# Issuing the Q and K weight loads from the scalar queue, with tiles 2 and 3 gated on tiles 0 and 1, in an attention-plus-GLU kernel

## The chip, the cores and the metric

The kernel runs on one core of a Trainium2 chip. The metric is the device time of one execution in microseconds (us).

Two numbers are used for one execution. The *time* is what is compared. The *span* runs from the first to the last instruction that the profile shows.

Engines are named as the profile names them: PE is TensorE, DVE is VectorE, ACT is ScalarE, POOL is GpSimd, SP is SyncE. "ACTq" or "SPq" is the instruction stream of that engine at work on issuing a DMA.

## The reference

One token tensor x of 2048 x 640 in bf16 is normalised. Two branches read the result and both are added to x.

```python
def reference(A_x, A_wqkv, A_wo, B_x, B_w_gate, B_w_up, B_w_down):
    def _A_ref(x, wqkv, wo):                    # 32 heads of 20, window of 8 positions, dilation 2
        # ... q, k, v from x @ wqkv; softmax over the window; weighted sum of v ...
        return o @ wo
    def _B_ref(x, w_gate, w_up, w_down):
        g = jnp.einsum("bsd,df->bsf", x, w_gate)
        u = jnp.einsum("bsd,df->bsf", x, w_up)
        return jnp.einsum("bsf,fd->bsd", g * u, w_down)
    x = A_x
    xn = _layernorm(x, axis=-1)
    return x + _A_ref(xn, A_wqkv, A_wo) + _B_ref(xn, B_w_gate, B_w_up, B_w_down)
```

## The kernel before

Tokens come in 16 tiles of 128. For the first tiles, the way to the first useful matmul is a chain over three engines: the tile lands; VectorE takes its statistics (two halves and an aggregate); ScalarE takes a square root, before which its stream has the load of a function table (1.28 us in the profile of before); VectorE takes the reciprocal and normalises; TensorE transposes; VectorE and ScalarE copy the transposed tile out of PSUM; TensorE multiplies it with the Q weights.

```python
def front(t):
    # ...
    yield have("x", t)
    if t == 1:
        yield have("sd", 0)
    for i in range(2):
        if t == 2 and i == 1:
            yield have("xnt", 1)
        yield Task("dve", lambda: stats(i), r=[x], prio=-1 if t == 1 and i == 0 else p)
    yield Task("dve", aggr, r=[("st", t, 1)], prio=p)
    yield Task("act", sqrt, r=[("mv", t)], prio=p - 1)          # "the root" below
    yield Task("dve", recip, r=[("sd", t)], prio=p)
    # ...
    yield Task("dve" if t < N_DVE_A else "act", apply, r=[("rstd", t), x], w=[xs], prio=p)   # normalise
    # ... five transposes on PE (trans), then the copy to XNT (part, copy) ...
```

The text of the program is not the order of the instructions. A scheduler in the kernel file runs when the program is built: it keeps a clock for each engine, models when each operation and each DMA ends, and appends the ready task of best priority to the engine's stream. On the chip that order is fixed, and in these traces an engine waits where an input is late, with what stands behind it: in e3 below, a reciprocal on VectorE whose root was done at 4.73 started only at 5.49, behind statistics that had waited 0.68 us for a tile. The DMA part of the model, with the program's own constants, is this:

```python
if dma:
    self.t[eng] = start + (0.48 if occ is None else occ)
    # ...
    self.t_data = max(self.t_data, start + 1.2) + nbytes / 280e3
    X.end = self.t_data + 0.8 + extra
```

These are the loads and the start of the program. `K.t["act"]` tells the model when ScalarE is free after its first issues and its table load.

```python
def x_load(t, eng="sp"):
    dma(XST[:, xslot(t), :], xhbm[t * TS:(t + 1) * TS, :], w=[XST[:, xslot(t), :]], name=f"xld{t}", eng=eng)
    mark("x", t)
# ...
def wqkv_load(g, lo=0, hi=NCH):
    dst = WQKV[:, WPOS[g], lo:hi, :]
    dma(dst, wqkv_src[:, lo:hi, g * D:(g + 1) * D], w=[dst], name=f"ld_wqkv{g}_{lo}")
# ...
x_load(0)
tch = A_wqkv.rearrange("(c k p) n -> k c p n", k=16, c=NCH)[:, :, 0, 0:32]
stores.append(dma(TCH[0:16], tch, w=[TCH[0:16]], name="touch", eng="act"))   # 5 KB that nobody reads
x_load(1)
wqkv_load(0, 0, 3)       # Q weights, first piece
wqkv_load(0, 3, NCH)     # Q weights, second piece
x_load(2)
wqkv_load(1, 0, 3)       # K weights
wqkv_load(1, 3, NCH)
x_load(3)
K.t["act"] = 2.1
warm(18)                 # 18 matmuls on zeros, before there is work for PE
```

Of the kernel before, what the change touches and what calls it, by code (L numbers as in the profile page):

```python
# [10 lines left out]
D = 640  # L11
NCH = 5
# [9 lines left out]
TS = 128  # L22
# [324 lines left out]
def build_kernel(nc, A_x, A_wqkv, A_wo, B_x, B_w_gate, B_w_up, B_w_down, out):  # L347
    K = Sched(nc)
# [4 lines left out]
    def sb(name, shape, dtype=BF16, at=None):  # L353
        n = mybir.dt.size(dtype)
        for s in shape[1:]:
            n *= s
        n = (n + 63) // 64 * 64
        if at is None:
            at = place[0]
            place[0] += n  # L360
        assert at + n <= 229344, (name, at + n)
        return K.sbuf(name, shape, dtype, at)
# [10 lines left out]
    NXS = 12  # L373
    XST = sb("XST", [128, NXS, D], at=a_ot + NCH * JB * 2)
# [43 lines left out]
    XNS = sb("XNS", [128, NXN, D], at=a_xr)  # L418
# [3 lines left out]
    MV = sb("MV", [128, NT, 2], FP32)  # L422
    SD = sb("SD", [128, NT, 4], FP32)
    DUM = sb("DUM", [128, 16], FP32)
    TCH = sb("TCH", [128, NCH, 32])
    ZERO = sb("ZERO", [128, JB])
    EPSC = sb("EPSC", [128, 16], FP32)
    IDENT = sb("IDENT", [128, 128])
# [15 lines left out]
    def mark(*k):  # L444
        done.add(k)
# [4 lines left out]
    def have(*k):  # L450
        return lambda: k in done
# [4 lines left out]
    xhbm = A_x[0]  # L456
    ohbm = out[0]

    def dma(o, i, r=(), w=(), name="", eng="sp", group=None):
        n = mybir.dt.size(o.dtype)  # L460
        for s in o.shape:
            n *= s
        return op(eng, lambda e: e.dma_start(o, i), r=r, w=w, dma=True, name=name, nbytes=n, group=group)  # L463
# [6 lines left out]
       r=[IDENT[:]], w=[IDENT[:]], name="ident", occ=0.4)  # L470
# [3 lines left out]
       r=[G[:]], w=[G[:]], name="g1", occ=0.3)  # L474
    op("pool", lambda e: e.affine_select(G[:], G[:], pattern=[[-4, H]], compare_op=ALU.is_ge,
                                         fill=0.0, base=0, channel_multiplier=1),
       r=[G[:]], w=[G[:]], name="g2", occ=0.3)
    op("pool", lambda e: e.memset(KT[:, :, 0:PAD], 0.0), w=[KT[:, :, 0:PAD]], name="kpad", occ=0.3)

    def xslot(t):  # L480
        return t + 4 if t < 8 else t - 8

    def x_load(t, eng="sp"):
        dma(XST[:, xslot(t), :], xhbm[t * TS:(t + 1) * TS, :], w=[XST[:, xslot(t), :]], name=f"xld{t}", eng=eng)
        mark("x", t)

    wqkv_src = A_wqkv.rearrange("(c p) n -> p c n", p=128)

    def wqkv_load(g, lo=0, hi=NCH):
        dst = WQKV[:, WPOS[g], lo:hi, :]  # L490
        dma(dst, wqkv_src[:, lo:hi, g * D:(g + 1) * D], w=[dst], name=f"ld_wqkv{g}_{lo}")

    def loads():
        def t(f, *a):
            return Task("sp", lambda: f(*a), prio=0)

        for t_ in range(4, NXS):
            yield t(x_load, t_)
        yield t(wqkv_load, 2)
        for t_ in range(NXS, NT):  # L500
            yield have("apply", t_ - NXS)
            yield t(x_load, t_)

        def w(T, src):
            dma(T[:], src.rearrange("(c p) n -> p c n", p=128), w=[T[:]], name="ld_w")

        def pads():
            z = ZERO[:, 0:PAD].unsqueeze(1).to_broadcast([128, NCH, PAD])
            dma(vscr[:, 0:PAD].rearrange("(c p) s -> p c s", p=128), z, r=[ZERO[:, 0:PAD]], w=[("vscr", "pad")], name="vpad")

        yield have("xnt", NT - 1)
        yield t(w, WG, B_w_gate)
        yield t(pads)
        yield t(w, WU, B_w_up)
# [107 lines left out]
    def warm(n):  # L622
        for _ in range(n):
            op("pe", lambda e: e.matmul(PS[:, 7, 0:QB], ZERO[:, 0:128], ZERO[:, 0:QB], start=True, stop=True),
               r=[ZERO[:]], w=[PS[:, 7, :]], name="warm", occ=0.2 if n > 3 else 0.12)
# [576 lines left out]
    stores = []  # L1202
# [76 lines left out]
    FIN_PRIO = 8  # L1279

    x_load(0)
    tch = A_wqkv.rearrange("(c k p) n -> k c p n", k=16, c=NCH)[:, :, 0, 0:32]
    stores.append(dma(TCH[0:16], tch, w=[TCH[0:16]], name="touch", eng="act"))
    x_load(1)
    wqkv_load(0, 0, 3)
    wqkv_load(0, 3, NCH)
    x_load(2)
    wqkv_load(1, 0, 3)
    wqkv_load(1, 3, NCH)
    x_load(3)  # L1290
    K.t["act"] = 2.1
    warm(18)

    def misc():
        yield have("xnt", NT - 1)

        def sel():
            for q in range(4):
# [6 lines left out]
                                     name="exp_preload", occ=1.3), prio=6)  # L1305

    K.spawn(loads())
    for t in range(NT):
        K.spawn(front(t))
# [20 lines left out]
def bass_parallel_sum__sliding_local_dilated__glu_gated_bilinear__prompt_kernel(  # L1330
    nc, A_x, A_wqkv, A_wo, B_x, B_w_gate, B_w_up, B_w_down, out
):
    build_kernel(nc, A_x, A_wqkv, A_wo, B_x, B_w_gate, B_w_up, B_w_down, out)
# [28 lines left out]
```

## Time and profile before

| kernel before | value |
|---|---|
| time, median of 3 runs | 270.04 us (269.69 to 270.15) |
| the profiled execution | 270.63 us, span 268.9 us, granted clock 1.0 |
| PE busy | 262.7 us, 98% of the span |
| first Q weight piece: issued, landed | 1.73, 7.17 us |
| first projection matmul | 7.30 us |

The table of stretches gives, for each window in us: its length, the busy time of each engine with its number of instructions (in the order PE, PE's weight loads, DVE, ACT, POOL), the granted clock, the busy share of the DMA engines and GB/s.

```profile
0.00:7.30 7.30, 5.37 (x26) 3.41 (x27) 3.71 (x13) 2.17 (x4) 1.30 (x10) 1.00 0.71 215
7.30:20.00 12.70, 12.09 (x195) 11.69 (x196) 8.87 (x26) 6.43 (x14) 0.00 (x0) 1.00 0.81 280
80.00:140.00 60.00, 59.58 (x311) 27.08 (x310) 50.61 (x56) 21.18 (x34) 28.89 (x15) 1.00 0.58 138
```

PE is full in the middle of the kernel. What can be won lies in the first 20 us. The next view is the chain of waits that ended last, in order of time, cut to its first part: start, length, and what was done. Pieces named "issue" of 0.05 us or less are left out of the chains shown. The weight piece is on it, from its issue to its landing.

```profile
1.73 5.44 DMA WQKV<-in_A_wqkv_dram
7.17 0.14 issue
7.30 0.84 PE PS L640 x12
8.16 0.62 PE PS L640 x8
8.78 0.29 PE PS L585 x5
9.09 0.50 DVE XNT L604
9.64 1.98 PE PS L640 x32
```

ScalarE's timeline shows the other side (start, length, engine, line, operation; in brackets the idle time before it and what ended it). The table load is over at 2.54, long before the first root is wanted; tile 0's share of the copy is done at 6.55.

```profile
0.83 0.40 ACTq L463 DMA_DIRECT2D TCH<-in_A_wqkv_dram  x1
1.26 1.28 ACT L544 ACT_TABLE_LOAD   x1 [1.26 <-PEq L1347]
4.38 0.30 ACT L544 ACTIVATE SD<-MV,EPSC 128x1 f32<-128x1 f32 x1 [1.84 <-DVE MV L541]
6.17 0.38 ACT L597 ACTIVATE XNT<-PS 128x256 bf16<-128x256 bf16 x1 [1.49 <-PE PS L585]
...
10.26 0.30 ACT L544 ACTIVATE SD<-MV,EPSC 128x1 f32<-128x1 f32 x1 [0.85 <-DVE MV L541]
```

### The profile page before, as it was taken

To read this page: it belongs to the slowest core of one execution; us is meant where nothing else is said; L and a number is where in the kernel's file an instruction comes from. 1 tells how busy PE (TensorE), PEld (TensorE's weight loads), DVE (VectorE), ACT (ScalarE), POOL (GpSimd) and SP (SyncE) were. 2 spreads that over 40 slices of the span, in tenths; PEclk is the share of its full clock that TensorE was granted. 3 is DMA by queue.
4 is the path that set the end of the run, shared out by engine and by line. 5 is a ranking of instruction groups with operands and counts; after the bars stand their busy time and mean duration, and the time that the engine had idled before them with its cause. 6 is when DMAs were issued, how large, how long until landed. Compare 5 with 4: busy or idle time off the path is not lost.

```text
span 268.9 us, 4464 instructions
## 1 busy us (share of the span) xinstructions
PE 262.7 (98%) x1765; PEld 152.8 (57%) x1783; DVE 222.9 (83%) x282; ACT 105.4 (39%) x188; POOL 130.3 (48%) x81
## 2 busy tenths in 40 slices
PE   7899999999999999999999999999999999999996
PEld 5796975444444444444444445765457654676775
DVE  4678899999999997379999899999999989992212
ACT  3369998556723232245344353024430342201000
POOL 1000000000004439900199999999999879985000
PEclk9999999999999999999999999999999999999999
DMA  6954479621414998087025953465534561022201
GB/s 206 367 188 74 98 105 339 247 97 56 142 39 113 234 244 177 0 268 151 2 52 140 240 118 79 132 176 138 152 79 130 148 195 42 27 73 61 87 28 49
DMA packets 40261, 35.58 MB, mean 132 GB/s; under 512 B 15408, under 2 KB 38448, under 8 KB 40240
## 3 DMA queue, kind: packets, MB, share of 16 engines
q1 hardware_dynamic: 39424, 33.15, 45.4%
q0 software_dynamic: 576, 2.10, 3.9%
q8 instruction: 14, 0.23, 0.4%
q10 hardware_dynamic: 240, 0.05, 0.1%
q14 instruction: 7, 0.06, 0.1%
HBM read 25.07 MB, written 5.26 MB: 113 GB/s over the span
## 4 chain that ended last, share of the span: by engine, by line
PE 94%; DMA 2%; DVE 2%; issue 1%; SPq 0%; DVEq 0%
PE PS L1149 36%; PE PS L1231 28%; PE PS L640 24%; PE PS L903 3%; DMA WQKV<-in_A_wqkv_dram 2%; PE PS L1098 2%; DVE HT L1158 1%; PE PS L585 0%; DVE RS L952 0%; DVE LOG L956 0%; SPq L463 0%; DVE XNT L604 0%; DVE SM L932 0%; DVE FOUT L1244 0%; DVEq L325 0%
## 5 line engine op out<-in xcount | busy, mean ns | idle before, releaser
L1056 POOL TENSOR_TENSOR SV<-PV 128x1024 bf16<-128x1024 f32 x40 | 93.5, 2366 | 24.7 <-DVE LOG L956 18.7
L1051 DVE TENSOR_TENSOR PV<-VX,PS 128x1024 f32<-128x1024 bf16 (+1 forms) x56 | 91.8, 1670 | 0.3 <-POOL SV L1056 0.3
L640 PE MATMUL PS<-XNT,WQKV 128*128 128x512 bf16 (+2 forms) x474 | 66.4, 299 | 1.6 <-DVE XNT L604 0.6
L1149 PE MATMUL PS<-XNT,WU 128*128 128x512 bf16 x239 | 59.6, 380 | 0.2
L1149 PE MATMUL PS<-XNT,WG 128*128 128x512 bf16 x229 | 57.3, 380 | 0.7 <-issue 0.3
L640 PEld LDWEIGHTS PS<-XNT,WQKV 128*128 128x128 bf16 x480 | 43.6, 113 | 23.8 <-DVE SD L549 1.0
L1149 PEld LDWEIGHTS PS<-XNT,WU 128*128 128x128 bf16 x240 | 23.3, 98 | 28.7 <-ACT XNT L645 0.8
L1149 PEld LDWEIGHTS PS<-XNT,WG 128*128 128x128 bf16 x240 | 23.2, 98 | 28.6 <-issue 0.8
L792 DVE TENSOR_TENSOR PRD<-QT,KT 128x2048 bf16<-128x2048 bf16 x32 | 36.8, 1217 | 0.0
L1244 DVE TENSOR_TENSOR FOUT<-PS,XR 128x320 bf16<-128x320 f32 (+1 forms) x33 | 15.7, 479 | 22.2 <-PE PS L1231 22.0
L1231 PE MATMUL PS<-WD,HT 128*128 128x320 bf16 x192 | 28.7, 300 | 0.0
L645 ACT ACTIVATE HT<-PS 128x512 bf16<-128x512 f32 x24 | 14.3, 596 | 34.0 <-PE PS L1149 34.0
L1231 PE MATMUL PS<-WO,OT 128*128 128x320 bf16 (+1 forms) x165 | 27.0, 296 | 0.0
L863 POOL TENSOR_TENSOR PRF<-PRF,PRF 128x1024 f32<-128x1024 f32 x4 | 9.4, 2352 | 33.1 <-DVE PRF L837 33.0
L1107 ACT ACTIVATE OT<-PS 128x512 bf16<-128x512 f32 x20 | 10.5, 600 | 34.4 <-PE PS L1098 34.4
L922 POOL MEMSET LOG<- 32x6 bf16 (+6 forms) x7 | 0.4, 95 | 48.4 <-ACT LOG L914 48.4
L1158 DVE TENSOR_TENSOR HT<-HT,PS 128x512 bf16<-128x512 bf16 x24 | 16.3, 680 | 8.7 <-PE PS L1149 7.0
L1231 PEld LDWEIGHTS PS<-WD,HT 128*128 128x128 bf16 x192 | 18.8, 98 | 7.6
L1231 PEld LDWEIGHTS PS<-WO,OT 128*128 128x128 bf16 x165 | 15.7, 98 | 6.6 <-issue 0.8
L837 DVE TENSOR_TENSOR PRF<-PS,KT 128x1024 f32<-128x1024 f32 x16 | 19.0, 1216 | 0.4 <-DMA PRF<-PRF 0.4
L538 DVE BATCH_NORM_STATS2 STATS<-XST 128x6 f32<-128x320 bf16 x32 | 14.7, 471 | 3.0 <-DMA XST<-in_A_x_dram 3.0
L1231 PE MATMUL PS<-WD,XNT 128*128 128x320 bf16 (+1 forms) x108 | 14.6, 285 | 0.0
(58 smaller groups left out, 216.1 us busy)
## 6 DMA issues: line engine op xcount, KB each, us to landing
VX<-v_scratch SPq DMA_DIRECT2D x80, 130.0 KB, 2.9
XST<-in_A_x_dram SPq DMA_DIRECT2D x16, 160.0 KB, 6.2
v_scratch<-VST SPq DMA_DIRECT2D x4, 640.0 KB, 4.3
XR<-in_A_x_dram SPq DMA_DIRECT2D x16, 160.0 KB, 2.9
out_dram<-FOUT SPq DMA_DIRECT2D x15, 160.0 KB, 1.8
PRF<-PRF POOLq DMA_DIRECT2D x4, 512.0 KB, 8.6
WG<-in_B_w_gate_dram SPq DMA_DIRECT2D x1, 1920.0 KB, 8.6
WU<-in_B_w_up_dram SPq DMA_DIRECT2D x1, 1920.0 KB, 12.1
```

What stands on the lines that cost most here:

```text
L538: op("dve", lambda e: e.bn_stats(o, a), r=[a], w=[("st", t, i)], name=f"bn{t}_{i}", occ=0.49)
L640: op("pe", (lambda o, l, x, c, first: lambda e: e.matmul(o, l, x, start=first, stop=(c == NCH - 1)))(o, l, x, c, first), r=[l, x], w=[o], ...
L645: X = op("act", (lambda o, i: lambda e: e.activation(o, i, ACT.Copy))(o, i), r=[i], w=[o], name=name, occ=0.12 + n * 0.9e-3)
L792: op("dve", lambda e: e.tensor_tensor(s[:], qb, kv, ALU.mult), r=[q, rk], w=[s[:]], name=f"prod{j}_{r}_{c}", occ=1.15, lock=True)
L837: X = op("dve", lambda e: e.tensor_tensor(o[:], qb, kv, ALU.mult), r=[q, rk], w=[o[:]], name=f"prow{j}_{r}_{c}_{q0}", occ=1.17)
L1051: op("dve", lambda e: e.tensor_tensor(p, vw, a, ALU.mult), r=[vv] + rk, w=[p], name=f"pv{u}_{x}_{r0}", occ=0.09 + 1.1 * nr)
L1056: X = op("pool", lambda e: e.tensor_tensor(o, p[:, :, 0, :], p[:, :, 1, :], ALU.add), r=[p[:]] + tokens(), w=[o], name=f"pva{u}_{x}", occ= ...
L1107: X = op("act", (lambda o, b: lambda e: e.activation(o, PS[:, b, :], ACT.Copy))(o, b), r=[PS[:, b, :]], w=[o], name=f"oev{u}", occ=0.58)
L1149: op("pe", (lambda l, x, c: lambda e: e.matmul(PS[:, b, :], l, x, start=(c == 0), stop=(c == NCH - 1)))(l, x, c), r=[l, x], w=[PS[:, b, :] ...
L1158: X = op("dve", lambda e: e.tensor_tensor(h, h, PS[:, hold[1], :], ALU.mult), r=[h, PS[:, hold[1], :]], w=[h], name=f"h{m}_{j}", occ=0.65)
L1231: op("pe", (lambda l, x, i: lambda e: e.matmul(dst, l, x, start=(i == 0), stop=(i == n - 1)))(l, x, i), r=[l, x], w=[PS[:, b, :]], name=f" ...
L1244: X = op("dve", lambda e: e.tensor_tensor(o, PS[:, b, 0:wid], xr, ALU.add), r=[PS[:, b, :], xr], w=[o], name=f"fin{t}_{nb}", occ=0.15 + wi ...
```

## The change

The intent is to get the weights sooner: SyncE issues only token tiles, and ScalarE issues the Q and K weights at once. Tiles 2 and 3 are loaded only when tiles 0 and 1 have been normalised, which is meant to keep them out of the weights' way. The touching read goes. `[EPSC[:]]` makes ScalarE's first issue wait for a memset, which ends at 1.24.

```diff
     def x_load(t, eng="sp"):
-        dma(XST[:, xslot(t), :], xhbm[...], w=[XST[:, xslot(t), :]], name=f"xld{t}", eng=eng)
+        r = [XNS[:, t - 2, :]] if 2 <= t < 4 else []
+        dma(XST[:, xslot(t), :], xhbm[...], r=r, w=[XST[:, xslot(t), :]], name=f"xld{t}", eng=eng)
 # ... wqkv_load gets eng= and r= ...
-        for t_ in range(4, NXS):
+        for t_ in range(2, NXS):
+            if t_ < 4:
+                yield have("apply", t_ - 2)
             yield t(x_load, t_)
 # ...
     x_load(0)
-    tch = A_wqkv.rearrange("(c k p) n -> k c p n", k=16, c=NCH)[:, :, 0, 0:32]
-    stores.append(dma(TCH[0:16], tch, w=[TCH[0:16]], name="touch", eng="act"))
     x_load(1)
-    wqkv_load(0, 0, 3)
-    wqkv_load(0, 3, NCH)
-    x_load(2)
-    wqkv_load(1, 0, 3)
-    wqkv_load(1, 3, NCH)
-    x_load(3)
-    K.t["act"] = 2.1
+    wqkv_load(0, 0, 3, "act", [EPSC[:]])
+    wqkv_load(0, 3, NCH, "act")
+    wqkv_load(1, 0, 3, "act")
+    wqkv_load(1, 3, NCH, "act")
+    K.t["act"] = 4.2
```

More of the change, by code (lines that the diff above doesn't have):

```diff
@@ L424, in build_kernel @@
     DUM = sb("DUM", [128, 16], FP32)
-    TCH = sb("TCH", [128, NCH, 32])
     ZERO = sb("ZERO", [128, JB])
@@ L483, in x_load, with wqkv_load @@
     def x_load(t, eng="sp"):
-        dma(XST[:, xslot(t), :], xhbm[t * TS:(t + 1) * TS, :], w=[XST[:, xslot(t), :]], name=f"xld{t}", eng=eng)
+        r = [XNS[:, t - 2, :]] if 2 <= t < 4 else []
+        dma(XST[:, xslot(t), :], xhbm[t * TS:(t + 1) * TS, :], r=r, w=[XST[:, xslot(t), :]], name=f"xld{t}", eng=eng)
         mark("x", t)
     wqkv_src = A_wqkv.rearrange("(c p) n -> p c n", p=128)
-    def wqkv_load(g, lo=0, hi=NCH):
+    def wqkv_load(g, lo=0, hi=NCH, eng="sp", r=()):
         dst = WQKV[:, WPOS[g], lo:hi, :]
-        dma(dst, wqkv_src[:, lo:hi, g * D:(g + 1) * D], w=[dst], name=f"ld_wqkv{g}_{lo}")
+        dma(dst, wqkv_src[:, lo:hi, g * D:(g + 1) * D], r=r, w=[dst], name=f"ld_wqkv{g}_{lo}", eng=eng)
     def loads():
```

## The prediction

> **What bounds it now.** TensorE. The page gives PE 262.7 us busy of a 268.9 us span (98%), and the chain that ended last is 94% PE. In the table of stretches PE is busy 59.6 of 60 us from 80 to 140 and again from 140 to 200. So the kernel can gain only where PE idles, and the change touches only the first 20 us. There the table shows 1.93 us idle before 7.30 (1.27 of it before the first warm-up matmul) and 0.61 us from 7.30 to 20. The opening chain (waits in order of time): SP issues x0 at 0.82, x1 at 1.27, the first Q weight piece at 1.73; that piece lands 5.44 us later, at 7.17, and the first projection matmul starts at 7.30. PE waits 0.5 us for it (waits view). The other input of that matmul, tile 0 transposed, was complete at 6.55 (timeline: ScalarE copy 6.17 + 0.38). So the weight piece is late by about 0.65 us; the rest of the start is the token chain: landing 3.2, statistics, root at 4.38, normalise 4.91, transpose 5.42, copies to 6.55.
>
> **What the change does.**
> - Q/K weights are issued by ScalarE after the memset that ends at 1.23, not by SP at 1.73: about 0.45 us earlier. [...] this 0.45 us is just that, the SP issue of x1 (0.40 us) being what is skipped.
> - Tile 2 (160 KB) no longer sits between Q and K weights, tile 3 no longer before tile 4; K weights, landing at 9.8 and 10.7 now, should land by about 8.5 to 9.5. Tile 2 is issued at about 5.4 and competes for the engines with the K weights, landing about 8.3 (8.5 now); tile 3 is issued at 7.5, landing about 10 (11.2 now).
> - ScalarE now issues four loads (0.43 to 0.49 us each by the trace) ahead of its table load (1.28 us): 1.26 + about 1.9 + 1.28 = 4.45, against a root that started at 4.38. So the token chain slips 0.1 us, more if an issue blocks (SP's later issues took 0.92 us).
> - The touching read (5 KB, landed at 3.4) goes. If it warmed the way to the weights, the first piece will be slower; in the trace 15 of its 16 engine completions were in by about 5.8 and one came at 7.17, so such stragglers exist even with it. I expect no large loss.
>
> **On the critical path.** First matmul at the later of tokens (about 6.7) and weight (5.3 to 6.8): I estimate 6.8, 0.5 us earlier. The 0.57 us gap before tile 1's projection (9.07 to 9.64, copy and transpose of tile 1) stays; its copy now goes ahead of tile 2's statistics, which helps slightly. Afterwards PE runs full, so the gain passes to the end. Reordering later (weight products among projections) moves nothing of PE's sum.
>
> **Predicted time**: 269.5 us (before 270.04), 268.7 to 270.3 eight times in ten. Faster by over 2%: 0.01; within 2%: 0.98; slower by over 2%: 0.01.
>
> **What would show it.** Right: first projection matmul at 6.6 to 7.0; its releaser ScalarE's or VectorE's tile 0 copy, not a weight; table load ending 4.3 to 4.6; K weights landed before 9.6; no PE wait for a token tile. PE busy sum unchanged within 1 us.
>
> **What would make it wrong.** ScalarE issue blocking past 5 us (root late); the first weight piece landing at 7.2 or later without the touch (gain zero or negative); tiles 2 to 4 starving PE at 12 to 16 us; a new wait in mid-kernel from the changed order of products.

One clause is cut where it is marked: a general reason for the 0.45 us, which no measurement of this case shows. No term of the prediction's sums goes with it: the root is still put at 1.26 + about 1.9 + 1.28 = 4.45, the first matmul 0.5 us earlier, the time at 269.5.

## More of the kernel before

The profiled execution was itself slower than the highest of the three timed runs.

PE reaches tile 3's transposes without a wait (no bracket):

```profile
14.54 0.45 PE L585 MATMUL PS<-IDENT,XNS 128*128 128x128 bf16 x5
```

## The result, and the profile after

The kernel after took 270.75 us (median of 6 runs, 270.55 to 270.96) where the kernel before took 270.12 us in the same rounds (6 runs, 269.69 to 270.40). The ratio is 1.0022, 95% interval [1.001, 1.0035]. A ratio here is the mean time of one kernel's fast runs over that of the other's of the same rounds, so it is not quite the ratio of the medians quoted. The result is correct, all runs were fast and the clock was 1.0 (0.999 in one). It is within 2%, as predicted, but on the wrong side of zero and outside the predicted range of 268.7 to 270.3.

The chain of waits of the kernel after, cut to its pieces up to tile 3, reads quite differently:

```profile
1.27 0.46 ACTq L462
...
2.81 0.51 ACTq L462
3.35 1.28 ACT L546
4.65 0.30 ACT SD L546
...
6.48 1.31 PE PS L642 x20
...
8.65 4.09 PE PS L642 x65
...
13.13 0.49 DVE XNT L606
13.62 0.41 DVE STATS L540
14.05 0.22 DVE MV L543
14.30 0.30 ACT SD L546
14.82 0.46 DVE XNS L558
15.32 0.45 PE PS L587 x5
```

Two things are to be seen. First, no DMA is left on it: the Q piece landed at 5.47 and the wait for it is gone. In its place stand ScalarE's four issues and then the table load, and the first root starts at 4.65, the moment the table is there (3.35 + 1.28 = 4.63). Second, there is a detour at 13.13 that the chain of before does not have: PE waits for tile 3, whose statistics stand behind a copy of tile 2 on VectorE. PE's timeline has that wait:

```profile
15.32 0.45 PE L587 MATMUL PS<-IDENT,XNS 128*128 128x128 bf16 x5 [0.34 <-DVE XNS L558]
```

PE's weight loads also waited 0.30 us, until 13.67, for that copy of tile 2. ScalarE's and VectorE's timelines show an ordering of the same kind for tile 2:

```profile
11.12 0.60 ACT L647 ACTIVATE KT<-PS 128x512 bf16<-128x512 f32 x1 [0.52 <-PE PS L642]
11.61 0.28 ACT L546 ACTIVATE SD<-MV,EPSC 128x1 f32<-128x1 f32 x1
```

```profile
9.97 0.21 DVE L543 BATCH_NORM_AGGREGATE MV<-STATS 128x2 f32<-128x12 f32 x1
11.93 0.16 DVE L551 RECIPROCAL SD<-SD 128x1 f32<-128x1 f32 x1 [1.75 <-ACT SD L546]
```

Tile 2's aggregate is done at 10.18 (9.97 + 0.21). Its root starts at 11.61, because a K evacuation stands before it in ScalarE's stream and waits for PE. The table of stretches:

```profile
0.00:7.30 7.30, 5.22 (x41) 3.71 (x42) 3.62 (x13) 2.26 (x4) 1.30 (x10) 1.00 0.74 240
7.30:20.00 12.70, 11.73 (x185) 10.85 (x183) 8.17 (x23) 5.83 (x14) 0.00 (x0) 1.00 0.85 262
```

From 7.30 to 20 PE is idle for 0.97 us (12.70 - 11.73), against 0.61 before. The span of the profiled run, 268.8, is the same as that of the profiled run of before, 268.9, though the times differ by 0.6 us in the median. Either the profiled run of before was not typical, or something lies outside the span. The experiments show both.

### The profile page after: what moved, and what is told of

Read it like the earlier page. It is cut to its first block, busy times and chain, and to the rows that moved or that the text cites. A ratio compares the mean times of both kernels' runs of the same rounds, so it can differ in the third digit from the quotient of the medians.

```text
span 268.8 us, 4476 instructions
## 1 busy us (share of the span) xinstructions
PE 263.3 (98%) x1783; PEld 152.2 (57%) x1783; DVE 223.1 (83%) x282; ACT 105.1 (39%) x188; POOL 130.3 (48%) x81
## 3 DMA queue, kind: packets, MB, share of 16 engines
q10 hardware_dynamic: 1488, 1.68, 1.8%
## 4 chain that ended last, share of the span: by engine, by line
PE 96%; DVE 1%; ACTq 1%; ACT 1%; issue 0%
PE PS L1151 39%; PE PS L1233 28%; PE PS L642 24%; PE PS L905 3%; PE PS L1100 2%; PE PS L587 1%; ACTq L462 1%; ACT L546 0%; DVE XNT L606 0%; DVE XNS L558 0%; ACT SD L546 0%; DVE STATS L540 0%; DVE SD L551 0%; PE PS L626 0%; DVE FOUT L1246 0%
## 5 line engine op out<-in xcount | busy, mean ns | idle before, releaser
L1151 PE MATMUL PS<-XNT,WG 128*128 128x512 bf16 x240 | 59.7, 379 | 0.0
```

Source lines behind the costliest of these rows:

```text
L1151: op("pe", (lambda l, x, c: lambda e: e.matmul(PS[:, b, :], l, x, start=(c == 0), stop=(c == NCH - 1)))(l, x, c), r=[l, x], w=[PS[:, b, :] ...
```

## The experiments

Fourteen kernels were run, in four batches; each batch shares its runs of the kernel before. All results were correct. Three theories stood at the start, and a fourth came out of the first batch.

- Theory A: the profiled execution of before was unlucky. Its late weight piece (one packet of 1280 bytes took 2.05 us in the trace's packet records) is not what a typical run has, so the change had less to win than the 0.65 us that the prediction read off.
- Theory B: four issues ahead of the table load delay the root by more than predicted.
- Theory C: taking the touching read away cost something.
- Theory D, later: the order that the scheduler fixed is what loses inside the kernel.

### The kernel before again, and the touching read

`e1_before_again` is the kernel before, unchanged, to get a second profile of it.

> The kernel before, unchanged, profiled and timed once more. Theory A (the first profile was unlucky: one stalled packet of 2.05 us made the first Q weight piece late, 7.17 us, and that execution took 270.63 against a median of 270.04): here the piece lands by about 5.8, the first projection matmul starts at 6.3 to 6.7, and the span is 268.1 to 268.5. Theory B (the piece is late in every execution of the kernel before): it lands again after 7.0, first projection at 7.2 or later, span 268.9. Theory C (the 0.6 us lie outside the span, before or after it): the span is again about 268.9 while the time stays at 270.1.

It took 270.04 us (269.86 to 270.98), ratio 1.0005 [0.9991, 1.0018], span of the profiled run 268.2. Its chain and PE's timeline:

```profile
1.73 4.68 DMA WQKV<-in_A_wqkv_dram
```

```profile
6.54 1.51 PE L640 MATMUL PS<-XNT,WQKV 128*128 128x128 bf16 x20 [0.48 <-DMA WQKV<-in_A_wqkv_dram]
```

The same DMA took 4.68 us instead of 5.44, and the first projection started at 6.54, not 7.30. Nor is this one profile the only evidence: the ten fast runs of before in the same rounds have spans of 267.8 to 268.6, against 268.9, and in the other kernels that issue this piece at 1.73 it landed at 6.29 (f3), 6.70 (f1) and 5.51 (f4). So the whole gain that the prediction saw (7.30 to 6.8) was there in an ordinary run of the kernel before. The kernel after starts its first projection at 6.48, earlier than e1 by 0.06 us. Theory A holds, though the piece landed at 6.41, not by 5.8: even an ordinary run of before waits about half a microsecond for it.

`f3_no_touch` is before without the touching read; `e2_touch_back` is after with it.

```diff
# f3, against before                       # e2, against after
-    stores.append(dma(TCH[0:16], tch, ... name="touch", eng="act"))
                                          +    stores.append(dma(TCH[0:16], tch, ... name="touch", eng="act"))
```

> The kernel before without its touching read; no other instruction changes. If the read prepares the way to the weights, the first Q piece lands later than with it (6.4 and 7.2 in the two profiles) and the time rises; theory A expects no effect beyond 0.2 us: ratio 0.9995 to 1.0008, span 268.0 to 268.5.

> The changed kernel with the touching read put back, issued by ScalarE at 0.83, in time in which ScalarE only waits for the memset; nothing else differs. If the missing touch costs the 0.6 us, this returns to about 270.1 (ratio 1.000), with the first Q piece landing under 5.3. Theory A: the weights are not what the first projection waits for in the changed kernel (5.48 landed, 6.48 started), so ratio 1.002 as without it, within 0.001.

f3 took 269.70 us, ratio 0.9997 [0.9985, 1.0009]; its Q piece landed at 6.29 and its first projection started at 6.42. e2 took 271.17 us, ratio 1.0047 [1.0028, 1.0066], one of its runs at 272.65; the Q piece landed at 5.42 and the first projection started at 6.58. Taking the touch away costs nothing measurable, and putting it back brings nothing. Theory C falls.

### ScalarE's issues ahead of the root

`e3_k_on_sp` leaves the Q weights on ScalarE and gives the K weights to SyncE, behind tile 1.

```diff
-    wqkv_load(1, 0, 3, "act")
-    wqkv_load(1, 3, NCH, "act")
+    wqkv_load(1, 0, 3)
+    wqkv_load(1, 3, NCH)
```

> The changed kernel with the two K weight pieces issued by SP after tile 1, so ScalarE issues two loads in place of four; the order of every compute engine is the same. Theory A: table load starts near 2.3 in place of 3.35, the root of tile 0 at about 4.37 in place of 4.65, first projection about 6.2, 0.25 us earlier. The gaps before tiles 2 and 3 stay, so the time falls by 0.1 to 0.3 us only (ratio about 1.0015). If the issue by ScalarE costs nothing, the time stays at 1.0022.

It took 272.02 us (271.67 to 273.09), ratio 1.0069 [1.0057, 1.0081]: a miss. The table load started at 2.29 and the root at 4.44, as expected of fewer issues. But tile 1 landed at 5.06 instead of 4.19, and VectorE's fixed order has the first half of tile 1's statistics in front of tile 0's reciprocal:

```profile
5.08 0.49 DVE L540 BATCH_NORM_STATS2 STATS<-XST 128x6 f32<-128x320 bf16 x1 [0.68 <-DMA XST<-in_A_x_dram]
5.49 0.15 DVE L551 RECIPROCAL SD<-SD 128x1 f32<-128x1 f32 x1
```

So tile 0 waited for tile 1, the first projection started at 7.33, and the second Q piece landed near 9.0. Loads on the other queue were not free for the rest: tile 1 (160 KB), which landed at 3.61 in before, landed at 4.19 in after and at 5.06 here. That loads of two queues are under way at once is in the packet records of after: from 3.0 to 4.0 us 79 packets of SyncE's queue and 135 of ScalarE's. By what rule the DMA engines share themselves out was not shown.

`e10_both` issues the K weights from ScalarE, but after the root of tile 0, and tells the scheduler's model that tiles 2 and 3 land 1 us earlier.

```diff
-    wqkv_load(1, 0, 3, "act")
-    wqkv_load(1, 3, NCH, "act")
-    K.t["act"] = 4.2
+    K.t["act"] = 3.2
+    def k_loads():
+        yield have("sd", 0)
+        yield Task("act", lambda: wqkv_load(1, 0, 3, "act"), prio=-5)
+        yield Task("act", lambda: wqkv_load(1, 3, NCH, "act"), prio=-5)
# and in x_load, for tiles 2 and 3:  X.end -= 1.0
```

> As e6, and the two K weight pieces issued by ScalarE after the root of tile 0 in place of before its table load; all compute orders are those of e6. Expected: table load at 2.3, root at 4.3 in place of 4.65, first projection near 6.15 in place of 6.48, K weights still in before 9.5; 0.3 us faster than e6, ratio to before about 0.999. If the issue cost of ScalarE is not on the path, it equals e6.

It took 271.08 us, ratio 1.0028 [1.0004, 1.0053]. The start was as expected: root at 4.38, first projection at 6.20. That is 0.28 us earlier than in after, so theory B holds: the last two issues were on the path. But now tile 2, which can be issued only when tile 0 is normalised (5.36), behind the K weights (issued from 4.39 on), came late: VectorE waited 1.89 us for it, and PE 1.60 us:

```profile
10.21 0.89 DVE L542 BATCH_NORM_STATS2 STATS<-XST 128x6 f32<-128x320 bf16 x2 [1.89 <-DMA XST<-in_A_x_dram]
```

```profile
12.41 0.45 PE L589 MATMUL PS<-IDENT,XNS 128*128 128x128 bf16 x5 [1.60 <-DVE XNS L560]
```

`e4_no_gate` is after without the gate: tiles 2 and 3 follow tiles 0 and 1 at once on SyncE. `e11_x2_early` has tile 2 right behind tile 1, only tile 3 gated, and the K weights after the root as in e10.

```diff
# e4, against after                        # e11, against after
-        r = [XNS[:, t - 2, :]] if 2 <= t < 4 else []
+        r = []                            +        r = [XNS[:, 0, :]] if t == 3 else []
     x_load(1)                                  x_load(1)
+    x_load(2)                             +    x_load(2)
+    x_load(3)                             # ... K weights as in e10
# ... and loads() begins at tile 4             # ... and loads() at tile 3
```

> The changed kernel without the gate: tiles 2 and 3, and then 4 to 11, issued by SP at once after tile 1. [...] Expected: Q pieces land at 6.5 and 8.5 in place of 5.5 and 6.4, K pieces after 11, TensorE waits about 1 to 2 us more, ratio 1.004 to 1.009. If the two rings do not slow each other, the Q pieces land as in the changed kernel and the time is 1.000 to 1.002.

> The changed kernel with tile 2 issued at once after tile 1, tile 3 gated on tile 0, and the K weights issued by ScalarE after the root of tile 0: an attempt to beat both. Expected: root at 4.35, Q pieces in by 6.0 and 7.0, first projection near 6.2, tile 2 landed by 5.5, K pieces by 8.9, no wait of TensorE over 0.5 us from there to 20; span 267.8 to 268.1, ratio to before 0.999 to 1.000. If tile 2 takes too much from the Q weights, the first projection starts at 6.5 or later and nothing is won.

e4 took 270.21 us, ratio 1.0025 [1.0012, 1.0038], where a larger loss was expected: a miss. (The reason given for the loss, cut where it is marked, was the author's estimate of how two queues share the bandwidth.) The gate seems worth little, but the scheduler planned e4 anew, with another order on every engine than in after, so the gate alone is not isolated. Its times include one of 271.23, the profiled run, in which PE's early matmuls were slow: the five transposes at 5.97 and at 8.39 took 0.71 and 0.74 us, those at 12.44 took 0.44. e11 took 270.11 us, ratio 1.0011 [0.9999, 1.0023]: the root at 4.41, the first projection at 6.59 (6.2 was expected), no large wait later. It is among the best of the versions with weights on ScalarE, and it does not beat before.

### The fixed order

`e5_root2_first` swaps two entries in ScalarE's stream: the root of tile 2 goes ahead of the K evacuation.

```diff
     K.run()
+    a_i = next(i for i, X in enumerate(K.ops) if X.name == "pev1_0")
+    b_i = next(i for i, X in enumerate(K.ops) if X.name == "sd2")
+    K.ops.insert(b_i, K.ops.pop(a_i))
     K.emit(stores)
```

> The changed kernel with one swap in ScalarE's order: the root of tile 2 ahead of the first K evacuation. Theory A: in the changed kernel that root started at 11.61 though its input was ready at 10.18, and TensorE then waited about 0.2 us for tile 2 (13.67) and 0.5 us for tile 3 (15.32). With the swap the root starts near 10.6, both gaps close, and the time falls by 0.5 to 0.7 us to about 270.1 (ratio 0.9995 to 1.0005). If the gaps do not reach the end, the ratio stays at 1.0022.

It took 270.90 us (270.77 to 272.81), ratio 1.0044 [1.0021, 1.0066], and its undisturbed runs are no better than after's: a miss. The root of tile 2 came at 10.64 instead of 11.61, but PE still waited for tile 3:

```profile
15.41 0.45 PE L587 MATMUL PS<-IDENT,XNS 128*128 128x128 bf16 x5 [0.34 <-DVE XNS L558]
```

```profile
13.21 0.49 DVE L606 COPY XNT<-PS 128x640 bf16<-128x640 bf16 x1 [1.19 <-PE PS L587]
13.62 0.48 DVE L540 BATCH_NORM_STATS2 STATS<-XST 128x6 f32<-128x320 bf16 x1
```

The second half of tile 3's statistics (13.62) stands behind the copy of tile 2 (13.21), and that copy waits for tile 2's transposes, which PE has behind 65 projection matmuls (8.80 to 12.73 in e5). One swap moved the wait to the next entry. This miss led to theory D: the order as a whole is wrong for the landings that the chip has. Two kernels test it in two ways. `e6_model_lands` leaves every DMA as in after and only tells the scheduler's model that tiles 2 and 3 land earlier by 2.0 and 1.5 us; with that, ScalarE's order of compute is exactly that of before, and PE's and VectorE's are nearly so (in the lists of the built programs, 5 of PE's 1783 entries and 2 of VectorE's 282 stand elsewhere). `e7_two_swaps` is e5 with tile 3's statistics also moved ahead of tile 2's copy; PE's order stays that of after. `e9_after_again` is after unchanged, beside them.

```diff
# e6, against after, in x_load
+        if t in (2, 3):
+            X.end -= (2.0, 1.5)[t - 2]
# e7, against e5
+    c_i = next(i for i, X in enumerate(K.ops) if X.name == "xntcp2")
+    for name in ("bn3_1", "bnag3"):
+        d_i = next(i for i, X in enumerate(K.ops) if X.name == name)
+        K.ops.insert(c_i, K.ops.pop(d_i))
+        c_i += 1
```

> The changed kernel with only the scheduler's guess of when tiles 2 and 3 land moved earlier by 2.0 and 1.5 us; loads, queues and gates are the same. ScalarE's order becomes that of the kernel before, TensorE's and VectorE's nearly so. Theory D (the loss is the new static order: the transpose of tile 2 behind 60 projections, tile 3's statistics behind tile 2's copy): both gaps close, span falls by 0.5 to 0.7 us against the changed kernel, ratio to before 0.9995 to 1.0005. Rival E (the loss is the loads themselves, gated tiles landing too late or the late root): the waits only move to other places and the ratio stays at 1.002.

> The changed kernel with two swaps: the root of tile 2 ahead of the first K evacuation on ScalarE (as in e5), and the second half of tile 3's statistics ahead of tile 2's copy on VectorE. Theory D: tile 3 is ready before TensorE asks, so the wait before its transpose (15.32, 0.34 idle) goes, the short one for tile 2 stays; the time falls by 0.3 to 0.5 us against the changed kernel, ratio to before 1.0005 to 1.0012. Rival E: no fall.

> The changed kernel again, unchanged, as the reference for this chip: ratio about 1.002. In its trace TensorE waits about 0.2 us for tile 2 and 0.5 us for tile 3 between 13 and 16 us. Its time should be about 2.0 us above its span, where the kernel before had 1.75.

e6 took 270.33 us, ratio 1.0008 [0.9986, 1.003], span 268.4. e7 took 270.38 us, ratio 1.0007 [0.9987, 1.0027], span 268.3. After itself, in e9, took 271.12 us, ratio 1.005 [1.0019, 1.0082]; two of its six runs were at 272.9 (below), and its other four had 270.80 to 271.23, spans 268.8 to 269.2; its profile, of one of the two, has the wait of 0.34 us for tile 3 at 17.38. In e6 and e7 PE reaches tile 3's transposes without a wait:

```profile
14.10 0.45 PE L589 MATMUL PS<-IDENT,XNS 128*128 128x128 bf16 x5
```

```profile
14.90 0.45 PE L587 MATMUL PS<-IDENT,XNS 128*128 128x128 bf16 x5
```

The first line is e6, the second e7; both had their first projection at 6.46, as after has it at 6.48. With the same DMAs and the same start, another order alone gives back about 0.6 us against the median of e9's four ordinary runs (270.95) and about 0.4 us against that of the first six runs of after (270.75). Eleven of the twelve runs of e6 and e7 lie at 270.24 to 270.63, below every run of e9; one of e6 took 271.21. Theory D holds for that part. It is not the whole of it, and e6 missed its expected ratio of 0.9995 to 1.0005 and its closing of both gaps. In e6 PE waits for tile 2 instead:

```profile
11.41 0.46 PE L589 MATMUL PS<-IDENT,XNS 128*128 128x128 bf16 x5 [0.34 <-DVE XNS L560]
```

The stretch from the first projection to the end of the span leaves the start out. It is 261.6 us in both profiles of before, 262.3 in after, 262.0 in e6 and 261.9 in e7. So the order is worth 0.3 to 0.4 of the 0.7 us lost there. What is left, about 0.3, is a wait for tile 2 in each. In e6, tile 2 landed at 9.19 and PE was there first, as rival E has it; in e1 it landed at 7.73, and PE did not wait for it. In e7, whose PE order is after's, the weight loads still wait 0.30 us for tile 2's copy, because its transposes stand behind the 65 projections and only 5 matmuls ahead of tile 2's own. Whether a better order would close this rest with tile 2 landing late was not tried; in e11, with tile 2 landed at 5.92 and another order, the stretch is 261.6.

### Two runs at 272.9

The profiled run of e9 is one of the two. Two things differ, both at the start. ScalarE's four issues took 2.48 us, not 2.06, and PE's matmuls took longer, up to the transposes at 9.39 (0.74 us).

```profile
1.27 2.48 ACTq L462 DMA_DIRECT2D WQKV<-in_A_wqkv_dram  x4
```

```profile
6.11 0.72 PE L587 MATMUL PS<-IDENT,XNS 128*128 128x128 bf16 x5 [0.81 <-DVE XNS L558]
...
7.25 2.34 PE L642 MATMUL PS<-XNT,WQKV 128*128 128x128 bf16 x20
```

The same five transposes took 0.45 us in after and the same 20 matmuls 1.31 us; here they took 0.72 and 2.34, longer by factors of 1.6 and 1.8. The 65 projection matmuls that follow, at 10.71, took 4.09 us, as in after. The granted clock reads 1.00 in this run too, so it does not show the slow matmuls, and what slowed them was not shown. The profiled runs of e3 (273.09) and e4 (271.23), each the slowest of its kernel, have slow matmuls too: 12 matmuls of the first projection in 1.49 us, against 0.88 in e11. In the profiles of after, e6 and e7 the 20 took 1.31, so slow matmuls do not make the difference between those. A run of this length still counts as fast, being less than 1.5% above the fastest, so it is in the means. Runs at 272.65 to 272.87 occurred once each in e2 and e5, twice in e9, and not in the first six runs of after; of these only this one has a profile, so that the others were slow in the same way is argued, not shown. Why after-like kernels had more of them than before was not tested.

### The weights without ScalarE's issues

`f7_tile1_on_act` takes the other way to the earlier weight: before, with tile 1 issued by ScalarE in the touch's place (but behind the memset, at 1.27), so that SyncE issues the Q weights 0.45 us earlier and ScalarE has one issue ahead of its table load. The order of the compute engines is that of before.

```diff
-    stores.append(dma(TCH[0:16], tch, w=[TCH[0:16]], name="touch", eng="act"))
-    x_load(1)
+    x_load(1, "act")
     wqkv_load(0, 0, 3)
# and in x_load, for tile 1:  r=[EPSC[:]]
```

> Before with one move: tile 1 is issued by ScalarE behind the memset, in the place of the touching read (which is gone), so SyncE issues the first Q weight piece 0.45 us earlier (1.27 instead of 1.73) and ScalarE spends only one issue (0.45 us) before its table load, not four (2.06). The static order of the compute engines is that of before. If the weight's wait at the start (about 0.35 to 0.5 us of PE in the runs of before) is really worth its length once neither the root nor the order pays for it: Q piece landed by 5.8, root at 4.3 to 4.4, first projection 6.1 to 6.3 against 6.5, span 0.2 to 0.4 us below before's, time less span 1.75, ratio 0.9985 to 0.9995. If the rival holds, that the Q piece lands when its neighbours in the queue let it and not by its issue: first projection 6.45 to 6.6 and ratio 1.000.

It took 270.21 us (269.51 to 270.61), ratio 1.0001 [0.9985, 1.0016]: no gain. The weight did land early, at 5.69, and PE no longer waited for it. But tile 1 landed at 4.71 instead of 3.61 as in before, and VectorE's order made tile 0 wait for it once more:

```profile
4.73 0.49 DVE L537 BATCH_NORM_STATS2 STATS<-XST 128x6 f32<-128x320 bf16 x1 [0.38 <-DMA XST<-in_A_x_dram]
5.14 0.15 DVE L548 RECIPROCAL SD<-SD 128x1 f32<-128x1 f32 x1
```

The first projection started at 6.62. Neither expectation named this: the weight came when its issue said, as the first theory had it, and the token paid, as it had in e3.

### What lies outside the span

The difference of time and span is 1.68 to 1.80 us in the runs of before, and 1.8 to 2.1 us in most runs of the kernels in which ScalarE issues all four weight pieces (after, e2, e4, e5, e6, e7, e9). In e11 and e10, where ScalarE issues the last two of the four after the first root, the medians are 1.95 and 1.85. It is 1.69 to 1.82 in e3, where ScalarE issues two. With medians of 1.75 and 2.0, about 0.25 us of the loss of 0.63 lies outside the span. Two kernels tried to find the cause. `f1_four_touches` is before with three more small reads on ScalarE (its order differs too, but only time less span is read from it); `f4_late_loads` is before without the touch, with ten loads of 128 descriptors each in ScalarE's stream at mid-kernel.

```diff
# f1, against before
+    for k in range(1, 4):
+        a = TCH[32 * k:32 * k + 16]
+        stores.append(dma(a, tch, w=[a], name=f"touch{k}", eng="act"))
# f4, against before: ten of these, placed between evacuations of the gate products
+        cols = DMP[:, 16 * n:16 * n + 16]
+        stores.insert(0, dma(cols, wqkv_src[:, 0, 16 * n:16 * n + 16], w=[cols], name=f"dump{n}", eng="act"))
```

> The kernel before with three more 5 KB touching reads issued by ScalarE at the start (four loads on its queue, as the changed kernel has, but hardly any bytes; the scheduler moves a few operations in its order as well). The kernels so far whose ScalarE issues four loads run about 2.0 us longer than their span, the others 1.75. If the number of loads on that queue makes the 0.25 us outside the span, time minus span is 2.0 here; if not, 1.75. Span: as before, 268.0 to 268.8.

> Before without the touching read, with ten loads of 128 descriptors each (32 B a descriptor, unread) put into ScalarE's stream at mid-kernel, where ScalarE has slack: 1,280 descriptors, as many as the four weight pieces have, on ScalarE's ring instead of none. If the number of descriptors issued by ScalarE makes the 0.25 us that the kernels with four weight pieces on ScalarE show outside the span: time less span 1.95 to 2.05 (before: 1.75) with a span within 0.3 us of before's, ratio about 1.001. If it is something else (the engine program's first microsecond, or bytes in flight at the start): time less span 1.70 to 1.80, ratio 1.000.

f1 took 270.04 us, ratio 1.001 [0.9997, 1.0023], and time less span was 1.69 to 1.75. f4 took 269.96 us, ratio 0.9996 [0.998, 1.0011], and time less span was 1.70 to 1.80. So neither four loads nor as many descriptors on ScalarE's queue are enough to make the difference; large loads at the start were not tried apart. The cause stays open.

f4 also shows why the start alone is not worth what it seems. In its profiled run the first projection started at 5.96, the earliest of all, and PE then waited for the next weights:

```profile
PE PS L640 <- DMA WQKV<-in_A_wqkv_dram: 0.8, 1, 0.8
```

(In the waits view: us in total, times, longest.) Its span was 268.4, that of before.

## Why the prediction was wrong

The claims, point by point:

- *PE bounds the kernel; only the first 20 us can change.* Right for the span. Not complete for the time: some 0.25 us appeared outside the span, which no view of the profile shows.
- *The weight piece is late by about 0.65 us.* Mis-sized. It was read from one execution, at 270.63 us while the median was 270.04. The second profile (e1) has the first projection at 6.54 with a wait of 0.48 us. The range 6.6 to 7.0 that the prediction called a success for after was already beaten by before.
- *The token chain slips 0.1 us.* Mis-sized. The prediction set ScalarE free at 4.45 and compared that with the root at 4.38 of the same unlucky run. Four issues took 2.06 us and the table load 1.28, from 1.27 on, so the root came at 4.65; in e1 it came at 4.25. That is 0.4 us, and e10 shows that the last two issues alone were worth 0.28 us at the first projection.
- *The first matmul comes 0.5 us earlier.* The sum of the two: 0.06 us earlier than in e1.
- *The 0.57 us gap before tile 1's projection stays.* Right: 0.58 in after, 0.59 in before.
- *The touching read is no large loss.* Right: f3 measured 0.9997.
- *K weights land before 9.6; no weight is waited for.* Right: they landed at 7.73 and 8.63, and no weight is on the chain.
- *Tile 2 lands at about 8.3 and tile 3 at about 10.* Tile 2 came 0.7 us later, at 9.03, tile 3 at 10.02. The 0.7 us were not harmless: see e6. (Both queues were at work then: from 7.5 to 8.5 us after's packet records have 141 packets of SyncE's queue, with the tiles, and 125 of ScalarE's, with the weights.)
- *"Afterwards PE runs full, so the gain passes to the end"; "Reordering later moves nothing of PE's sum"; "no PE wait for a token tile".* This is the step that failed. The gate moved the landing of tile 2 in the scheduler's model by 2.9 us, from 7.50 to 10.41 (the model's numbers, read out while the program is built); on the chip it moved from 8.46, or 7.73 in e1, to 9.03. So the scheduler put tile 2's root behind a K evacuation, tile 2's transposes behind 65 projections, and tile 3's statistics behind tile 2's copy. On the chip tile 2 was there 1.4 us before the model's time, and PE waited in an order made for other landings. e6 and e7 change the order and nothing else, and bring the median span from 268.7 (268.8 to 269.2 in e9's ordinary runs) to 268.4 and 268.35, where before had a median of 268.3 in the same rounds. What they leave, about 0.3 us from the first projection on, is again a wait for tile 2: from its late landing in e6, from PE's order in e7. PE's sum of work did not move, as the prediction said; its waits did. The prediction had named "tiles 2 to 4 starving PE" as a risk, but as one of late data, not of order, and gave it no share in the predicted time; the order could be read before the run.

The account, an estimate from these numbers: the predicted gain of 0.54 us was nearly zero (0.06 us at the first projection), the order cost about 0.4 us, the wait for tile 2 that is left up to 0.3, and 0.25 us lies outside the span. Together that is 1.1 to 1.4, where 1.25 us lie between the predicted 269.5 and the measured 270.75.

What limits the start, as far as these runs show it, is that an input that came earlier was paid for by another, and that the fixed orders tie them together. With the Q weight brought forward, tile 1 came later (3.61 in before, 5.06 in e3, 4.71 in f7); with the K weights issued after the root, VectorE waited 1.89 us for tile 2 (e10); and where everything for the first projection came early, the next weight was waited for (0.8 us in f4). No version tried beats before clear of the noise.

## What to carry to other kernels

Before a wait of half a microsecond is counted as a gain, compare the profiled execution's time with the median of the timed runs; if it is above them, its waits may be too (here 270.63 against 270.04 us, with the first projection at 7.30 against 6.54 in the second profile), and a second profile of the same kernel is the cheapest experiment there is. A DMA issue takes time in the stream of the engine that makes it (0.46 to 0.51 us each on ScalarE in after, 2.06 us for the four): place it by what that engine must do next (here a table load and a root), not only by how early the transfer starts. And where a scheduler fixes each engine's order from modelled landings, a change to a load changes the order of work far from it, so compare the orders on every engine, and check the modelled landings against the measured ones, before predicting that "nothing else moves".
